# Taking one row of a weight load off half of the DMA engines, and re-cutting the tail of a decode kernel around it

## The chip, the cores and the metric

The kernel runs on one core of a Trainium2 chip. The metric is the device time of one execution in microseconds (us), several executions per kernel. Each execution also lists the *span* of the core, from its first to its last recorded work. Where differences of a few tenths of a microsecond are argued, this document uses medians of spans beside the times.

## The reference, cut to what matters

The kernel computes `x + A(ln(x)) + B(ln(x))` for one token of 1024 values. A is attention over a cache of 65,536 keys with 4 key/value heads and 32 query heads. B is an MLP:

```python
def _B_ref(x, w1, w2, w3, w4):
    ...                                        # x1 = x + a small mixer; with one token the mixer's taps are zero
    h2 = _gelu(_layernorm(x1) @ w3) @ w4       # w3: 1024 x 3584, w4: 3584 x 1024, bf16
    return x1 + h2
```

The cache and the weights are 170 MB, read once. Last comes `w4`: 3584 rows of 1024 bf16 values (2 KB each), 28 rows for each of the 128 SBUF partitions.

## The kernel before

Everything is streamed into three large tiles over one DMA queue. `w4` comes last, in pieces, so that its matmuls can start on the early ones:

```python
W4_PIECES = (8, 12, 5, 2, 1)     # rows per partition of each load, sum 28
FIRST = 3
AT_ONCE = 1
NARROW = 8
AHEAD = 5
...
            elif it == "w4":
                w4_v = B_w4.rearrange("(m c) n -> m c n", c=FC)
                c0 = 0
                for n in W4_PIECES:
                    go(out=t[:, c0 * D:(c0 + n) * D], in_=w4_v[:, c0:c0 + n, :].rearrange("p c n -> p (c n)"))
                    c0 += n
```

A *wide* row is two matmuls of 512 columns, accumulated in the PSUM tile `psB`. The last eight rows are *narrow*: four matmuls of 256 columns in four column groups of the PE array, accumulated in two other PSUM tiles. So two engines copy the result out of PSUM at the end, one half each (0.37 us on ACT and 0.43 on DVE, side by side, for 64x256 values each; the add over 64x512 values that writes `sums` took DVE 0.68). What had been summed in `psB` until then (the other rows, the attention's projection of the last group, the residual) has to be brought over. It is copied to SBUF and added to the narrow tiles by two f32 matmuls with a selection matrix. I call these the *injection*.

```python
    compute_v(NU - 1)
    early = sum(W4_PIECES[:AT_ONCE])
    compute_w4(0, FIRST)
    ...
    projected = project(HKV - 1)
    with tc.issue_after(projected):
        compute_w4(early, FC - NARROW)                        # wide rows
    sums = ogpool.tile([64, 512], F32, name="sums", tag="og")
    nc.vector.tensor_tensor(out=sums[:], in0=psB[0:64, :], in1=tail["o"], op=ALU.add)
    ...
    narrow_rows(FC - NARROW, FC - NARROW + AHEAD, start=True) # the 5-row piece
    ...
    for h in range(2):                                        # the injection
        nc.tensor.matmul(quarters[h][64 * h:64 * h + 64, 0:256], lhsT=pick[:].rearrange("p j r -> p (j r)"),
                         rhs=sums[:, 256 * h:256 * (h + 1)], start=False, ...)
    narrow_rows(FC - NARROW + AHEAD, FC)                      # the 2-row and the 1-row piece
    out_t = ogpool.tile([64, 2, 256], BF16, name="out_t", tag="og")
    nc.scalar.copy(out=out_t[:, 0, :], in_=quarters[0][0:64, 0:256])
    nc.vector.tensor_copy(out=out_t[:, 1, :], in_=quarters[1][64:128, 0:256])
    ...                                                       # store
```

## Time and profile before

| | |
|---|---|
| time, median of the first 3 runs | 401.07 us (400.98 to 402.7) |
| span of the profiled run | 398.6 us |
| load queue, share of 16 engines' time | 98.9% |
| last `w4` landing | 396.44 us |
| start of the last four matmuls | 396.48 us |

The part of the page on DMA queues (queue and kind: packets, megabytes, share of the time of 16 engines) shows what bounds the kernel:

```profile
q1 hardware_dynamic: 4128, 169.87, 98.9%
q8 instruction: 9, 0.15, 0.2%
q14 instruction: 1, 0.01, 0.0%
```

The load queue leaves the DMA engines 1.1% of free time. The other two lines look negligible: nine packets of 16 KB and one of 8 KB. The profile marks all ten as instruction packets (0.98 to 1.10 us for each of the first eight of 16 KB, 0.33 for the one of 8 KB); what the one of 8 KB holds is not shown.

The chain of waits ends like this (start, us, what):

```profile
363.32 33.11 DMA big<-in_B_w_dram
396.44 0.04 issue
396.48 0.34 PE pm_r L501 x4
396.82 0.02 issue
396.84 0.43 DVE out_t L522
```

PE waits for the last load and needs 0.34 us after it. From the start of the last four matmuls to the end of the span are 2.12 us (398.60 - 396.48).

The windows near the end, of which the last two columns are read here (share of the DMA engines that are busy, GB/s):

```profile
394.00:394.50 0.50, 0.25 (x4) 0.00 (x0) 0.21 (x1) 0.00 (x0) 0.00 (x0) 1.00 0.87 344
394.50:395.00 0.50, 0.41 (x16) 0.40 (x20) 0.47 (x1) 0.00 (x0) 0.00 (x0) 1.00 0.55 221
395.00:395.50 0.50, 0.50 (x14) 0.23 (x8) 0.00 (x0) 0.00 (x0) 0.00 (x0) 1.00 0.53 205
395.50:396.00 0.50, 0.50 (x12) 0.17 (x9) 0.00 (x0) 0.00 (x0) 0.00 (x0) 1.00 0.32 119
```

From 394.5 on only about half of the engines still move data (0.55 and 0.53), and then fewer. Each of these loads has 16 landings among the trace's semaphore events, as many as the page counts DMA engines. Read as one landing for each engine, they say which part of them is late. Here are the 16 landings of four loads, as us before the last of the 16 (the trace does not name the engines, the values are sorted):

```
lands at  22.0: 0.63 0.53 0.46 0.43 0.37 0.35 0.34 0.33 0.29 0.26 0.25 0.19 0.18 0.16 0.13 0.00
lands at  50.0: 1.92 1.81 1.74 1.70 1.66 1.63 1.62 1.61 1.57 1.56 1.48 1.47 1.46 1.40 1.30 | 0.00
lands at 166.1: 1.98 1.87 1.81 1.75 1.70 1.69 1.64 1.63 1.55 1.53 1.46 1.38 | 0.72 | 0.18 0.05 0.00
lands at 396.4: 1.96 1.82 1.66 1.54 1.53 1.47 1.37 | 0.71 | 0.31 0.24 0.18 0.17 0.16 0.09 0.05 0.00
```

The first load ends evenly. Then one engine after another falls 1.3 us back (1.30 in the second row), and the eight 16 KB instruction packets before the end (42.5, 105.9, 156.9, 198.0, 253.4, 296.9, 338.0 and 383.8 us) are just as many as the late engines. One engine falls 0.7 us back at the 8 KB packet (113.2 us; of the landings that end at 108.1 us none stands between the two groups, of those that end at 127.4 one does, 0.66 us after the early ones). At the end eight engines are late, one half late, seven early.

### The profile page before, as it was taken

The numbers are of one execution on the slowest core, as the hardware profiler recorded it, in microseconds if no ns is written. First come the engines' busy times: TensorE is split into PE (matmuls) and PEld (weight loads), VectorE is DVE, ScalarE is ACT, GpSimd is POOL, SyncE is SP. The second block draws the span as 40 slices with busy tenths as digits, with TensorE's granted clock in tenths as the row PEclk, the third lists the DMA queues.
The fourth block names the chain that finished last, engine by engine and source line by source line (L and its number), as shares of the span: only waits on it lengthen the run. The fifth ranks groups of instructions, "written<-read, shape, count | busy, mean of one in ns | idle before, by whom it ended". The sixth has DMA issues, their size and how long they took to land.

```text
span 398.6 us, 2575 instructions
## 1 busy us (share of the span) xinstructions
PE 225.4 (57%) x1360; PEld 44.0 (11%) x866; DVE 210.7 (53%) x160; ACT 27.1 (7%) x35; POOL 5.8 (1%) x29
## 2 busy tenths in 40 slices
PE   0251960591569238733974296519462955394986
PEld 0210000010100010011001010200020101010132
DVE  0610010974296559633963795269439942894141
ACT  1001020003000200020002000200110001002000
POOL 2000000000000000000000000000000000000000
PEclk9995996596869787966695889679956896698799
DMA  9998999999999999999999999999999998999996
GB/s 421 421 443 376 446 427 480 454 421 421 416 428 427 421 467 449 427 421 427 423 441 421 447 454 434 416 427 421 441 436 427 447 447 383 416 462 424 413 432 257
DMA packets 4144, 170.03 MB, mean 427 GB/s; under 512 B 419, under 2 KB 421, under 8 KB 678
## 3 DMA queue, kind: packets, MB, share of 16 engines
q1 hardware_dynamic: 4128, 169.87, 98.9%
q8 instruction: 9, 0.15, 0.2%
q14 instruction: 1, 0.01, 0.0%
q10 hardware_dynamic: 6, 0.00, 0.0%
HBM read 169.87 MB, written 0.00 MB: 426 GB/s over the span
## 4 chain that ended last, share of the span: by engine, by line
DMA 56%; DVE 21%; PE 17%; ACT 2%; another core or an unknown queue 2%; issue 1%; SPq 0%; DVEq 0%; ACTq 0%
DMA big<-in_A_k_cache_dram 42%; DVE big L360 15%; PE sc L365 11%; DMA big<-in_B_w_dram 8%; DMA big<-in_A_wq_dram 6%; PE oacc L415 4%; DVE p_sb L386 2%; DVE mx L370 2%; ACT p_sb L383 2%; PE psq L290 1%; SPq L187 0%; PE pm_mx L372 0%; DVE m L374 0%; PE pm_mx L379 0%
## 5 line engine op out<-in xcount | busy, mean ns | idle before, releaser
L365 PE MATMUL sc<-big,qdiag 128*128 128x512 bf16 x512 | 129.6, 414 | 66.5 <-DVE big L360 61.0
L360 DVE STREAM_TRANSPOSE big<-big 128x4096 f32<-128x4096 f32 x32 | 139.4, 4413 | 50.1 <-DMA big<-in_A_k_cache_dram 50.1
L415 PE MATMUL oacc<-big,p_sb 128*32 128x512 bf16 x512 | 43.2, 504 | 34.5 <-DVE p_sb L386 34.5
L370 DVE TENSOR_REDUCE mx<-sc 128x1 f32<-128x2048 f32 x8 | 18.3, 2292 | 29.9 <-PE sc L365 29.9
L365 PEld LDWEIGHTS <-qdiag 128*128 128x128 bf16 x128 | 13.2, 103 | 178.3 <-issue 145.7
L383 ACT ACTIVATE p_sb<-sc,nball 128x2048 bf16<-128x2048 f32 x8 | 15.7, 1968 | 220.8 <-DVE nball L381 220.8
L386 DVE STREAM_TRANSPOSE p_sb<-p_sb 128x2048 bf16<-128x2048 bf16 x8 | 18.5, 2311 | 18.0 <-ACT p_sb L383 18.0
L415 PEld LDWEIGHTS <-p_sb 128*32 128x32 bf16 x512 | 16.2, 122 | 58.2 <-DVE p_sb L386 35.1
L290 PE MATMUL psh<-big,ln_rep_b 128*32 128x512 bf16 (+1 forms) x64 | 12.4, 942 | 8.9 <-DMA big<-in_B_w_dram 8.9
L455 PE MATMUL o_acc<-big,oT 128*1 128x512 bf16 x48 | 13.2, 447 | 2.4 <-ACT p_sb L383 2.4
L372 PE MATMUL pm_mx<-ident_f,mx 128*1 128x128 f32 x8 | 2.4, 296 | 19.1 <-DVE mx L370 19.1
L424 DVE SCALAR_TENSOR_TENSOR og<-oacc,wb,og 128x512 f32<-128x512 f32 x4 | 3.0, 751 | 18.5 <-PE oacc L415 18.5
L329 DVE STREAM_TRANSPOSE h_row<-h_row 128x896 bf16<-128x896 bf16 x1 | 1.1, 1111 | 22.0 <-ACT h_row L328 22.0
L241 PE MATMUL pm_ln<-ln_rowsum_a,ones_f 128*128 128x1 f32 x2 | 0.6, 348 | 12.8 <-DVE ln_rowsum_a L239 12.8
L437 PE MATMUL pm_e<-ol,sel8big 128*128 128x129 f32 x8 | 2.3, 370 | 9.7 <-DVE ol L436 9.7
L314 POOL COPY qdiag<-qx 32x32 bf16<-32x32 bf16 x16 | 3.3, 204 | 278.7 <-PE sc L365 250.7
L290 PE MATMUL psq<-big,ln_rep_a 128*32 128x512 bf16 x64 | 5.0, 479 | 3.7 <-DMA big<-in_A_wq_dram 3.7
L232 DVE STREAM_TRANSPOSE x_t<-x_row 32x256 bf16<-32x256 bf16 x4 | 2.5, 615 | 8.4 <-DMA x_row<-in_A_x_dram 8.3
L466 DVE TENSOR_TENSOR big<-o_acc,big 1x512 f32<-1x512 f32 x2 | 1.4, 679 | 10.3 <-PE o_acc L455 10.3
L227 PE MATMUL psB<-big,hT 128*32 128x512 bf16 x40 | 4.8, 380 | 1.4 <-DMA big<-in_B_w_dram 1.3
L302 DVE CAST q_row<-psq 128x512 bf16<-128x512 f32 x1 | 0.7, 692 | 7.6 <-PE psq L290 7.6
L379 PE MATMUL pm_mx<-ident_f,rep 1*128 1x1 f32 x8 | 1.8, 229 | 5.0 <-DVE rep L376 5.0
(100 smaller groups left out, 71.9 us busy)
## 6 DMA issues: line engine op xcount, KB each, us to landing
big<-in_A_wo_dram SPq DMA_DIRECT2D x1, 8192.0 KB, 35.7
big<-in_B_w_dram SPq DMA_DIRECT2D x1, 7168.0 KB, 38.1
big<-in_B_w_dram SPq DMA_DIRECT2D x3, 2048.0 KB, 35.5
big<-in_B_w_dram SPq DMA_DIRECT2D x1, 3072.0 KB, 29.5
big<-in_B_w_dram SPq DMA_DIRECT2D x1, 1280.0 KB, 32.2
big<-in_B_w_dram SPq DMA_DIRECT2D x1, 512.0 KB
big<-in_B_w_dram SPq DMA_DIRECT2D x1, 256.0 KB, 33.1
big<-in_A_k_cache_dram SPq DMA_DIRECT2D x8, 42.2
```

The lines of the kernel that those rows point to most:

```text
L227: return nc.tensor.matmul(psB[32 * j:32 * j + 32, :], lhsT=lhsT.to_broadcast([lhsT.shape[0], 32]), rhs=rhs, start=start, stop=False, tile_ ...
L232: nc.vector.transpose(out=x_t[32 * a:32 * a + 32].rearrange("p c j -> p (c j)"), in_=x_row[:, 256 * a:256 * (a + 1)].rearrange("p (i c) -> ...
L290: nc.tensor.matmul(acc[32 * q:32 * q + 32, i, 0:n], lhsT=rep[:, c, :], rhs=cols(c, i, q), start=(c == 0), stop=(c == DC - 1), tile_positio ...
L314: nc.gpsimd.tensor_copy(out=qdiag[at, LEAD:].rearrange("p (x c) -> p x c", x=4)[:, :, 32 * a:32 * a + 8], in_=qx[at, :, 8 * g:8 * g + 8])
L360: nc.vector.transpose(out=words, in_=words)
L365: nc.tensor.matmul(sc[:, e, :], lhsT=qdiag[:, c0:c0 + P], rhs=cols[:, s, e, :, b2, :, r], start=(s == 0 and b2 == 0 and r == 0), stop=(s = ...
L370: nc.vector.reduce_max(out=mx[:], in_=sc[:].rearrange("p e n -> p (e n)"), axis=AX.X)
L383: nc.scalar.activation(out=p_sb[:], in_=sc[:], func=ACTF.Exp, bias=nball[:, b:b + 1], scale=SCALE, accum_out=group["lall"][:, b:b + 1])
L386: nc.vector.transpose(out=flat, in_=flat)
L415: mm = nc.tensor.matmul(oacc[32 * q:32 * (q + 1), :], lhsT=pT[:, e, 32 * t:32 * (t + 1)], rhs=vt[:, :, e, t, :], start=(e == 0 and t < 4), ...
L424: nc.vector.scalar_tensor_tensor(out=og[:], in0=oacc[:], scalar=wb[:, 1:2], in1=og[:], op0=ALU.mult, op1=ALU.add)
L455: nc.tensor.matmul(tail["rows"][0:1, h2, :], lhsT=oT[g][:, j:j + 1], rhs=wt[:, g, j, 512 * h2:512 * (h2 + 1)], start=(g == 0 and j == 0), ...
```

## The change

It means to even this out. The 28th row of each partition (128 rows of 2 KB, 8 for each engine) is no longer loaded by all 16 engines. It comes in seven small loads of 3, 3, 3, 5, 8, 8 and 8 partitions (below: the *shares*). The plan counts on a load on k partitions running on k engines, and on the larger of these loads using the engines of the smaller ones too. The engines are numbered here by this nesting alone: 0 to 2 are those of the loads of 3, each larger load adds the next ones, and 8 to 15, the "upper" ones, get no share. So engines 0 to 2 get 25 of the rows, 3 and 4 get 13, 5 to 7 get 9, and 8 to 15 none.

The values of `h` that multiply these scattered rows are put in their places by four small matmuls early on. The tail is re-cut too. The residual is injected before the 12-row piece. Of the sum only the first half is injected, and the second half is added in the final copy. Only six rows are narrow, and the pieces are 9, 12, 5 and 1. The core of the diff:

```diff
-W4_PIECES = (8, 12, 5, 2, 1)
-FIRST = 3
-AT_ONCE = 1
-NARROW = 8
+W4_PIECES = (9, 12, 5, 1)
+LEFT = 4
+SHARES = ((3, 0, 4), (3, 1, 4), (3, 2, 4), (5, 3, 4), (8, 32, 4), (8, 33, 4), (8, 34, 1))
+WHOLE = 27
+FIRST = 6
+NARROW = 6
 AHEAD = 5
...
+                nc.gpsimd.memset(t[:, WHOLE * D:(WHOLE + LEFT + 1) * D].bitcast(F32), 0.0)
+                c0, m0 = 0, 0
+                for share in SHARES[:3] + W4_PIECES[:1] + SHARES[3:] + W4_PIECES[1:]:
...
+                    k, i0, m = share           # k partitions, every fourth from i0, m rows each
+                    go(out=t[i0:i0 + 4 * k:4, WHOLE * D:(WHOLE + m) * D].rearrange("e (i n) -> e i n", i=m),
+                       in_=w4_v[m0:m0 + k * m, WHOLE, :].rearrange("(i e) n -> e i n", e=k))
...
-    nc.vector.tensor_tensor(out=sums[:], in0=psB[0:64, :], in1=tail["o"], op=ALU.add)
...
+    with tc.issue_after(projected):
+        for h in range(2):
+            begun = inject(h, pick[:].rearrange("p j r -> p (j r)"), tail["o"][0:64, 256 * h:256 * (h + 1)], True)
+    with tc.issue_after(begun):
+        compute_w4(early, WHOLE - NARROW)
+    nc.scalar.copy(out=sums[0][:], in_=psB[0:64, 0:256])
+    nc.vector.tensor_copy(out=sums[1][:], in_=psB[0:64, 256:512])
...
+    narrow_rows(WHOLE - NARROW, WHOLE - NARROW + AHEAD)
+    inject(0, ident_f[0:64, 0:64], sums[0][:], False)
+    narrow_rows(WHOLE - NARROW + AHEAD, WHOLE)
...
-    nc.vector.tensor_copy(out=out_t[:, 1, :], in_=quarters[1][64:128, 0:256])
+    nc.vector.tensor_tensor(out=out_t[:, 1, :], in0=quarters[1][64:128, 0:256], in1=sums[1][:], op=ALU.add)
```

More of the change, by code (lines that the diff above doesn't have):

```diff
@@ L126 @@
     assert DH == P and HQ // HKV == 8 and HKV == 4 and D == 1024 and F == 3584 and S == 1
-    assert SK % UKEYS == 0 and sum(W4_PIECES) == FC
+    assert SK % UKEYS == 0 and sum(W4_PIECES) == WHOLE == FC - 1
     NB = SK // UKEYS
@@ L184, in load @@
                 w4_v = B_w4.rearrange("(m c) n -> m c n", c=FC)
-                c0 = 0
-                for n in W4_PIECES:
-                    go(out=t[:, c0 * D:(c0 + n) * D], in_=w4_v[:, c0:c0 + n, :].rearrange("p c n -> p (c n)"))
-                    c0 += n
+                nc.gpsimd.memset(t[:, WHOLE * D:(WHOLE + LEFT + 1) * D].bitcast(F32), 0.0)
+                c0, m0 = 0, 0
+                for share in SHARES[:3] + W4_PIECES[:1] + SHARES[3:] + W4_PIECES[1:]:
+                    if share in W4_PIECES:
+                        go(out=t[:, c0 * D:(c0 + share) * D], in_=w4_v[:, c0:c0 + share, :].rearrange("p c n -> p (c n)"))
+                        c0 += share
+                        continue
+                    k, i0, m = share
+                    go(out=t[i0:i0 + 4 * k:4, WHOLE * D:(WHOLE + m) * D].rearrange("e (i n) -> e i n", i=m),
+                       in_=w4_v[m0:m0 + k * m, WHOLE, :].rearrange("(i e) n -> e i n", e=k))
+                    m0 += k * m
+                assert m0 == P and c0 == WHOLE
             else:
@@ L284 @@
         nc.vector.tensor_copy(out=x_halves[32 * j:32 * j + 1, :], in_=x_row[0:1, 512 * j:512 * (j + 1)])
+    place = ogpool.tile([P, LEFT, P], BF16, name="place", tag="og")
+    nc.gpsimd.memset(place[:], 0.0)
+    m0 = 0
+    for k, i0, m in SHARES:
+        cells = place[:, 0:m, i0:i0 + 4 * k:4].rearrange("p i e -> p e i")
+        nc.gpsimd.affine_select(out=cells, in_=cells, compare_op=ALU.not_equal, fill=1.0, base=-m0,
+                                pattern=[[-1, k], [-k, m]], channel_multiplier=1)
+        m0 += k * m
     def row_matmul(acc, rep, cols, widths):
@@ L316, in place_queries @@
                 in_=qx[at, :, 8 * g:8 * g + 8])
-    hT = const.tile([P, FC], BF16, name="hT")
+    hT = const.tile([P, WHOLE + LEFT], BF16, name="hT")
+    h_left = const.tile([P, 1], BF16, name="h_left")
     def compute_w3():
@@ L329, in compute_w3, with place_left @@
         nc.vector.transpose(out=h_row[:], in_=h_row[:])
-        nc.vector.tensor_copy(out=hT[:], in_=h_row[:, ::32])
+        nc.vector.tensor_copy(out=hT[:, 0:WHOLE], in_=h_row[:, 0:32 * WHOLE:32])
+        nc.vector.tensor_copy(out=h_left[:], in_=h_row[:, 32 * WHOLE:32 * WHOLE + 1])
+    def place_left():
+        pm = ps_M.tile([P, 512], F32, name="pm_h", tag="pm")
+        for x in range(LEFT):
+            nc.tensor.matmul(pm[:, x:x + 1], lhsT=place[:, x, :], rhs=h_left[:],
+                             start=True, stop=True)
+        nc.vector.tensor_copy(out=hT[:, WHOLE:], in_=pm[:, 0:LEFT])
     def compute_w12():
@@ L403, with compute_v @@
     assert NB == 2
-    def compute_v(u):
+    def compute_v(u, fill=None):
         g, b = divmod(u, NB)
@@ L425, in compute_v, with group_rows @@
                                        op0=ALU.mult, op1=ALU.add)
-        group_rows(g, og, ol)
-        return mm.ins
+        group_rows(g, og, ol, fill and (lambda: fill(mm.ins)))
     oT = {}
     tail = {}
-    def group_rows(g, og, ol):
+    def group_rows(g, og, ol, fill):
         pe = ps_M.tile([P, 512], F32, name="pm_e", tag="pm")
@@ L436, in group_rows @@
         nc.vector.tensor_reduce(out=ol[:, 0:DH], in_=og[:].rearrange("p (s d) -> p d s", d=DH), axis=AX.X, op=ALU.add)
-        tail["gathered"] = nc.tensor.matmul(pe[:, 0:DH + 1], lhsT=sel8big[:], rhs=ol[:], start=True, stop=True).ins
+        if fill is None:
+            nc.tensor.matmul(pe[:, 0:DH + 1], lhsT=sel8big[:], rhs=ol[:], start=True, stop=True)
+        else:
+            with tc.issue_after(fill()):
+                tail["gathered"] = nc.tensor.matmul(pe[:, 0:DH + 1], lhsT=sel8big[:], rhs=ol[:], start=True, stop=True).ins
         msk = small.tile([P, 16, 8], F32, name="msk", tag="msk")
@@ L460, in copy_projection @@
     def copy_projection():
-        tail["o"] = st.tiles["w4"][0:64, FC * D:FC * D + D].bitcast(F32)
-        nc.vector.tensor_scalar(out=tail["o"], in0=x_halves[:], scalar1=ln_s1[0:64, 0:1], scalar2=ln_s2[0:64, 0:1],
+        tail["o"] = st.tiles["w4"][:, (WHOLE + LEFT) * D:(WHOLE + LEFT + 1) * D].bitcast(F32)
+        nc.vector.tensor_scalar(out=tail["o"][0:64, :], in0=x_halves[:], scalar1=ln_s1[0:64, 0:1], scalar2=ln_s2[0:64, 0:1],
                                 op0=ALU.mult, op1=ALU.add)
@@ L471, in compute_w4 @@
             for j in range(2):
-                row_acc(j, hT[:, c:c + 1], wt[:, D * c + 512 * j:D * c + 512 * (j + 1)])
+                mm = row_acc(j, hT[:, c:c + 1], wt[:, D * c + 512 * j:D * c + 512 * (j + 1)])
+        return mm.ins
     compute_wq()
@@ L476 @@
     compute_w12()
+    place_left()
     for u in range(NU - 1):
@@ L484 @@
     copy_projection()
-    compute_v(NU - 1)
-    early = sum(W4_PIECES[:AT_ONCE])
-    compute_w4(0, FIRST)
-    with tc.issue_after(tail["gathered"]):
-        compute_w4(FIRST, early)
-    projected = project(HKV - 1)
-    with tc.issue_after(projected):
-        compute_w4(early, FC - NARROW)
-    sums = ogpool.tile([64, 512], F32, name="sums", tag="og")
-    nc.vector.tensor_tensor(out=sums[:], in0=psB[0:64, :], in1=tail["o"], op=ALU.add)
-    quarters = [ps_M.tile([P, 512], F32, name="pm_r", tag="pm") for _ in range(2)]
@@ L497, in quarter_acc, with first_rows @@
-    def quarter_acc(lhsT, rhs, start=False):
-        for h in range(2):
-            for j in range(2):
-                q = 2 * h + j
-                nc.tensor.matmul(quarters[h][32 * q:32 * q + 32, 0:256], lhsT=lhsT(j), rhs=rhs(j, h), start=start, stop=False,
-                                 tile_position=(0, 32 * q), skip_group_check=True)
-    def narrow_rows(lo, hi, start=False):
+    early = W4_PIECES[0]
+    def first_rows(summed):
+        with tc.issue_after(summed):
+            return compute_w4(0, FIRST)
@@ new lines @@
+    compute_v(NU - 1, first_rows)
+    with tc.issue_after(tail["gathered"]):
+        filled = compute_w4(FIRST, early)
+    with tc.issue_after(filled):
+        filled = compute_w4(WHOLE, WHOLE + LEFT)
+    with tc.issue_after(filled):
+        projected = project(HKV - 1)
+    quarters = [ps_M.tile([P, 512], F32, name="pm_r", tag="pm") for _ in range(2)]
+    sums = [ogpool.tile([64, 256], F32, name="sums_a", tag="og"), ppool.tile([64, 256], F32, name="sums_b", tag="p")]
+    pick = small.tile([64, 2, 32], F32, name="pick", tag="msk")
@@ new lines, with inject @@
+    nc.vector.tensor_copy(out=pick[:], in_=ident_f[0:64, 0:64].rearrange("p (j r) -> p j r", r=32)[:, :, 0:1].to_broadcast([64, 2, 32]))
+    def inject(h, lhsT, rows, start):
+        return nc.tensor.matmul(quarters[h][64 * h:64 * h + 64, 0:256], lhsT=lhsT, rhs=rows, start=start,
+                                stop=False, tile_position=(0, 64 * h), skip_group_check=True).ins
+    with tc.issue_after(projected):
+        for h in range(2):
+            begun = inject(h, pick[:].rearrange("p j r -> p (j r)"), tail["o"][0:64, 256 * h:256 * (h + 1)], True)
@@ L505, in narrow_rows @@
+    with tc.issue_after(begun):
+        compute_w4(early, WHOLE - NARROW)
+    nc.scalar.copy(out=sums[0][:], in_=psB[0:64, 0:256])
+    nc.vector.tensor_copy(out=sums[1][:], in_=psB[0:64, 256:512])
+    def narrow_rows(lo, hi):
         wt = st.tiles["w4"]
         for c in range(lo, hi):
-            quarter_acc(lambda j: hT[:, c:c + 1].to_broadcast([P, 32]),
-                        lambda j, h: wt[:, D * c + 512 * j + 256 * h:D * c + 512 * j + 256 * (h + 1)],
-                        start=start and c == lo)
@@ L511 @@
-    narrow_rows(FC - NARROW, FC - NARROW + AHEAD, start=True)
-    pick = small.tile([64, 2, 32], F32, name="pick", tag="msk")
-    nc.vector.tensor_copy(out=pick[:],
-                          in_=ident_f[0:64, 0:64].rearrange("p (j r) -> p j r", r=32)[:, :, 0:1].to_broadcast([64, 2, 32]))
-    for h in range(2):
-        nc.tensor.matmul(quarters[h][64 * h:64 * h + 64, 0:256], lhsT=pick[:].rearrange("p j r -> p (j r)"), rhs=sums[:, 256 * h:256 * (h + 1)], start=False,
-                         stop=False, tile_position=(0, 64 * h), skip_group_check=True)
@@ L518 @@
-    narrow_rows(FC - NARROW + AHEAD, FC)
+            for h in range(2):
+                for j in range(2):
+                    q = 2 * h + j
+                    nc.tensor.matmul(quarters[h][32 * q:32 * q + 32, 0:256], lhsT=hT[:, c:c + 1].to_broadcast([P, 32]),
+                                     rhs=wt[:, D * c + 512 * j + 256 * h:D * c + 512 * j + 256 * (h + 1)], start=False, stop=False,
+                                     tile_position=(0, 32 * q), skip_group_check=True)
+    narrow_rows(WHOLE - NARROW, WHOLE - NARROW + AHEAD)
```

## The prediction

> **What bounds the kernel.** The DMA stream: the DMA view shows the load queue busy for 98.9% of 16 engines' span, 170 MB at 427 GB/s; the chain of waits ends in 33.1 us of w4 loads (363.3 to 396.4), 0.34 us of matmuls, 0.43 us of output copy and the store. Only the last microseconds can move.
>
> **What is unbalanced there.** In windows of 0.25 us the DMA share is 0.83 to 0.98 until 394.5, then about 0.53 until 395.75: half the engines have finished. The 16 landings of the last w4 load agree: seven at 394.47 to 395.07, one at 395.73, eight at 396.13 to 396.44. The first load's spread is only 0.63 us; the late group grows by one engine after each of eight 16 KB packets of the instruction queue (42.5 to 383.8; 1.0 to 1.1 us each). So instruction fetches made the skew. [...] 222 to 320 PE instructions between them.
>
> **What the change does.** It takes the 28th row (2 KB a partition, 8 per DMA engine) off all 16 engines and gives 25, 25, 25, 13, 13, 9, 9, 9 rows to the lowest eight. A 2 KB packet starts every 0.080 us in the last load.
> - Upper eight: 8 rows less, 0.64 us earlier (396.44 to 395.8), if they are the late ones, which the trace does not name.
> - Lowest three: 17 rows more, +1.36 us. They led by 1.4 to 2.0 us, so they now end 0.0 to 0.6 us before the old end.
> So the last landing moves by 0.1 to 0.64 us, about 0.45.
>
> **What it gives back.** Only one row (0.65 us) now lies between the landings of the 5-row and the last piece, before three (394.55 to 396.44). After the 5-row landing PE does 20 narrow matmuls (0.66 us) and one f32 injection (half of 0.58, 0.29), so it reaches the last four matmuls about 0.35 us after the last landing; before it was 0.04. Loss 0.3 us. The output copy becomes an add of 64x256, near the old 0.43.
>
> **Off the critical path.** Pool's zeroing of 128x2560 before the first w4 issue (estimate 2.5 us from 0.54 for 128x536) and eleven w4 issues (0.42 each, some waiting for earlier landings): V's last load covers DMA until 379, the 9-row piece 5.5 us more. Eight more 512-wide matmuls before the last projection (0.9 us; PE had waited 1.3 us for the 12-row piece, which now lands 0.6 later); the residual, now behind the shares, is ready near 390.4, the 12-row piece near 392. 13 more PE instructions make no ninth fetch (188 follow the eighth).
>
> **Prediction.** 0.45 gained less 0.3: about 0.2 us. 400.9 us, 8 in 10 between 400.2 and 401.7; faster by over 2% 0.005, within 2% 0.985, slower by over 2% 0.01.
>
> **What would show it.** The stretch of half DMA share shrinks from 1.3 us to under 0.7; the last load's landings close up; PE works without a gap from the 5-row landing on.
>
> **What would make it wrong.** The early engines are not the lowest eight, or the three with 25 rows not the earliest: the end comes up to 1 us later. A late w4 issue starves the queue near 380. The residual's wait on all shares delays the injection past the 12-row landing. An extra fetch in the tail.

(A clause is cut where marked. No term of the sum goes with it: 0.45 us gained less 0.3, about 0.2. "Lowest" and "upper" are the numbers by nesting from above; that the engines called the lowest are the early ones was the author's assumption.)

## The result

The changed kernel took 401.5 us (median of 6, 401.09 to 401.69), the kernel before 401.05 us beside it (median of 6, 400.88 to 402.7). The ratio is 1.0004, with a 95% interval of 0.9988 to 1.002: the same. (Such a ratio is the mean time of one kernel's runs over that of the other's of the same rounds, so it is not quite the ratio of the medians. Here the single run of 402.7 us hides a part of the difference.) The spans are clearer: 399.0 to 399.3, median 399.05, against a median of 398.7 in three later sets of 9 to 11 runs of the kernel before. So the change costs about 0.35 us of span. That is inside the predicted range, and on the other side of zero from the predicted gain of 0.2. The range reached from a gain of 0.85 us to a loss of 0.65 us, so it held although both terms of the sum were off.

The queues of the changed kernel:

```profile
q1 hardware_dynamic: 4150, 169.87, 98.8%
q8 instruction: 9, 0.15, 0.1%
q14 instruction: 1, 0.01, 0.0%
```

The bytes are the same, with 22 more small packets. The end of its chain of waits:

```profile
380.49 15.15 DMA big<-in_B_w_dram
395.64 0.04 issue
395.68 0.73 PE pm_r L553 x20
396.41 0.57 PE pm_r L536 x2
396.98 0.28 PE pm_r L553 x4
397.26 0.02 issue
397.28 0.42 DVE out_t L563
```

The chain no longer ends with a load. It leaves DMA at 395.64, which is the landing of the 5-row piece, and from there on all is PE: 20 narrow matmuls, the injection, the last four. (The chain counts the work from the end of what came before. By the timeline, the last four start at 396.91.) The same windows as above:

```profile
394.00:394.50 0.50, 0.50 (x8) 0.23 (x4) 0.00 (x0) 0.00 (x0) 0.00 (x0) 1.00 0.76 315
394.50:395.00 0.50, 0.50 (x8) 0.27 (x5) 0.00 (x0) 0.00 (x0) 0.00 (x0) 1.00 0.63 250
395.00:395.50 0.50, 0.36 (x4) 0.06 (x1) 0.00 (x0) 0.11 (x1) 0.00 (x0) 1.00 0.47 176
395.50:396.00 0.50, 0.32 (x12) 0.32 (x15) 0.21 (x1) 0.26 (x1) 0.00 (x0) 1.00 0.13 49
```

The stream ends a little earlier (0.13 in place of 0.32 in the last window), but it still fades over 1.5 us. The landings of the last load, in us before 396.27:

```
2.15 2.02 1.78 | 1.22 | 0.83 0.76 0.66 0.59 0.55 0.51 0.37 | 0.13 0.13 0.10 0.08 0.00
```

The last landing came only 0.17 us earlier (396.44 to 396.27), in one trace of each kernel. And PE, which had started its last four matmuls 0.04 us after the last landing, now starts them 0.64 us after it (396.91 - 396.27). The sum is -0.17 + 0.60 = +0.43 us at the last four matmuls (396.48 to 396.91).

The two timelines of PE from the landing of the 5-row piece on show where the 0.60 comes from. Before:

```profile
394.59 0.73 PE L501 MATMUL pm_r<-big,hT 128*32 128x256 bf16 x20 [0.34 <-DMA big<-in_B_w_dram]
395.25 0.65 PE L516 MATMUL pm_r<-sums,pick 64*64 64x256 f32 x4
395.83 0.40 PE L501 MATMUL pm_r<-big,hT 128*32 128x256 bf16 x8
396.48 0.29 PE L501 MATMUL pm_r<-big,hT 128*32 128x256 bf16 x4 [0.24 <-DMA big<-in_B_w_dram]
```

After:

```profile
395.68 0.73 PE L553 MATMUL pm_r<-big,hT 128*32 128x256 bf16 x20 [0.32 <-DMA big<-in_B_w_dram]
396.34 0.64 PE L536 MATMUL pm_r<-sums_a,ident_f 64*64 64x256 f32 x2
396.91 0.29 PE L553 MATMUL pm_r<-big,hT 128*32 128x256 bf16 x4
```

Before, PE had 1.89 us between the landings of the 5-row and the last piece (394.55 and 396.44) and even waited. After, the two landings are 0.63 us apart (395.64 and 396.27), while PE needs 0.66 us for 20 matmuls and then 0.57 us for the injection. One injection takes 396.34 to 396.91. Two of them had taken 395.25 to 395.83. They stand in different column groups and ran side by side (0.58 us for two, 0.57 for one), so dropping one saved nothing.

### The profile page after: what moved, and what is told of

Same layout as the page of the kernel before. It is cut to its first block, busy times and chain, and to the rows that moved or that the text cites. A ratio compares the mean times of both kernels' runs of the same rounds, so it can differ in the third digit from the quotient of the medians.

```text
span 399.0 us, 2630 instructions
## 1 busy us (share of the span) xinstructions
PE 230.1 (58%) x1368; PEld 45.8 (11%) x874; DVE 210.9 (53%) x162; ACT 27.4 (7%) x36; POOL 10.0 (3%) x38
## 4 chain that ended last, share of the span: by engine, by line
DMA 51%; DVE 23%; PE 19%; ACT 3%; another core or an unknown queue 2%; issue 1%; SPq 0%; DVEq 0%; ACTq 0%
DMA big<-in_A_k_cache_dram 32%; DVE big L387 15%; PE sc L392 11%; DMA big<-in_A_v_cache_dram 10%; PE oacc L442 6%; DMA big<-in_A_wq_dram 5%; DMA big<-in_B_w_dram 4%; DVE p_sb L413 3%; DVE mx L397 3%; ACT p_sb L410 3%; PE psq L308 1%; PE pm_mx L399 0%; DVE m L401 0%; ACT L410 0%
## 5 line engine op out<-in xcount | busy, mean ns | idle before, releaser
L442 PE MATMUL oacc<-big,p_sb 128*32 128x512 bf16 x512 | 45.4, 525 | 34.5 <-DVE p_sb L413 34.5
L237 PE MATMUL psB<-big,hT 128*32 128x512 bf16 x50 | 5.9, 380 | 1.9 <-DMA big<-in_B_w_dram 1.9
L448 ACT COPY og<-oacc 128x512 f32<-128x512 f32 x4 | 2.3, 586 | 33.3 <-PE oacc L442 24.3
```

The source lines that it names most:

```text
L237: return nc.tensor.matmul(psB[32 * j:32 * j + 32, :], lhsT=lhsT.to_broadcast([lhsT.shape[0], 32]), rhs=rhs, start=start, stop=False, tile_ ...
L442: mm = nc.tensor.matmul(oacc[32 * q:32 * (q + 1), :], lhsT=pT[:, e, 32 * t:32 * (t + 1)], rhs=vt[:, :, e, t, :], start=(e == 0 and t < 4), ...
```

## The experiments

Two questions were open. First: is the late end PE work after the 5-row landing (theory P), or are the landings themselves, or the small loads, the cost (rivals D and S)? Second: why did the last landing move by only 0.17 us, and is the fetching of instructions really what makes engines late (theory F), rather than their place (rival U)? Each experiment has a profile. The table is the whole result; "lag" is the time from the last landing to the start of the last four matmuls, "span" the median of all executions of that kernel (six, but five for e9 and e10 and two for e7; of the kernel before, the later sets).

| kernel | 5-row landing | last landing | last four start | lag | span, median | time, median |
|---|---|---|---|---|---|---|
| before | 394.55 | 396.44 | 396.48 | 0.04 | 398.7 | 401.05 |
| changed | 395.64 | 396.27 | 396.91 | 0.64 | 399.05 | 401.5 |
| e1_gap | - | 396.31 | 396.60 | 0.29 | 398.75 | 401.2 |
| e2_bf16 | 396.06 | 396.71 | 396.98 | 0.27 | 399.1 | 401.33 |
| e3_even | 395.75 | 396.39 | 398.19 | 1.80 | 400.3 | 402.33 |
| e4_pieces | 395.89 | 396.53 | 397.17 | 0.64 | 399.2 | 401.48 |
| e5_early | 395.72 | 396.56 | 396.60 | 0.04 | 398.45 | 400.77 |
| e6_level | 396.38 | 397.02 | 397.44 | 0.42 | 399.4 | 401.57 |
| e7_fetch | 395.94 | 397.84 | 397.88 | 0.04 | 400.05 | 402.23 |
| e8_even_early | 395.71 | 396.35 | 396.39 | 0.04 | 398.7 | 400.75 |
| e9_five | 395.76 | 396.40 | 396.45 | 0.05 | 398.7 | 400.76 |
| e10_after_again | 395.60 | 396.22 | 396.87 | 0.65 | 399.0 | 401.61 |

The landings are of one profiled execution each, and they scatter. The five traces with the change's own deal (changed, e1, e2, e5, e10) have their last landing at 396.22 to 396.71, the four with an even deal (before, e3, e4, e8) at 396.35 to 396.53. So the landings alone do not show that the shares made the last one earlier. The spans of most kernels scatter by 0.2 to 0.4 us, apart from single outliers; those of e6 by 0.9. The sets of e1 to e4, of e5 to e8 and of e9 and e10 each ran on a chip of their own, with the kernel before at a median span of 398.7 beside each.

### e1_gap: the old spacing of the last pieces

```diff
-W4_PIECES = (9, 12, 5, 1)
+W4_PIECES = (9, 12, 3, 2, 1)
-AHEAD = 5
+AHEAD = 3
```

> The changed kernel with its 5-row piece cut into 3 and 2 rows (pieces 9, 12, 3, 2, 1; the injection after the 3 rows), so that it has the last-two-pieces spacing of the kernel before; shares kept. Theory P (the end of the changed kernel is PE work that starts at the 5-row landing, 1.27 us of it before the last four matmuls): the last four matmuls again wait for the last landing, which stays near 396.3, and the kernel gains about 0.6 us on the changed one (near 400.85, 0.15 to 0.2 under the kernel before). Rival D (the last landing decides and the shares cost or gain by themselves what was measured): no change from the changed kernel, 401.45.

It gained 0.3 us of span on the changed kernel, half of what theory P expected, and rival D is out. The trace names the missing half. The injection, moved forward, came at 395.80, when its input was just ready (the copy of `psB` had run from 395.38 to 395.74). That copy waits for 24 wide matmuls of 2.77 us that start with the 12-row landing at 392.54. So a second chain, which starts one piece earlier, lay close behind the first. In the kernel before, the 12-row piece had landed at 391.44, because two rows less came before it.

### e2_bf16: a cheaper injection

```diff
-    sums = [ogpool.tile([64, 256], F32, name="sums_a", tag="og"), ...
+    ident_b = const.tile([64, 64], BF16, name="ident_b")
+    nc.vector.tensor_copy(out=ident_b[:], in_=ident_f[0:64, 0:64])
+    sums = [ogpool.tile([64, 256], BF16, name="sums_a", tag="og"), ...
-    inject(0, ident_f[0:64, 0:64], sums[0][:], False)
+    inject(0, ident_b[:], sums[0][:], False)
```

> The changed kernel with the one injected partial sum and its identity in bf16 in place of f32 (rounds the partial sum once more on purpose). Theory P: the injection, 0.57 us from its start to that of the last four matmuls, shrinks to about 0.1 to 0.15, so the last four start near 396.45, and the kernel gains 0.4 to 0.45 us on the changed one (near 401.05, level with the kernel before). Rival D: no change, 401.45.

The time did not move: span 399.1. By its own term the theory held, as the timeline shows:

```profile
396.10 0.73 PE L555 MATMUL pm_r<-big,hT 128*32 128x256 bf16 x20 [0.33 <-DMA big<-in_B_w_dram]
396.76 0.29 PE L538 MATMUL pm_r<-sums_a,ident_b 64*64 64x256 bf16 x1
396.98 0.29 PE L555 MATMUL pm_r<-big,hT 128*32 128x256 bf16 x4
```

From the injection to the last four are 0.22 us, before 0.57. But in this execution the 5-row landing came at 396.06, 0.42 us later than in the profiled run of the changed kernel, and took the gain back. Whether the landings of this build are always that late is not known. Five of its six spans lie between 398.9 and 399.2, so chance in one run would not explain it. A miss for the forecast, and not a decision between the theories.

### e3_even: no shares, the changed tail

```diff
-W4_PIECES = (9, 12, 5, 1)
-LEFT = 4
-SHARES = ((3, 0, 4), ...)
-WHOLE = 27
+W4_PIECES = (10, 12, 5, 1)
+LEFT = 0
+SHARES = ()
+WHOLE = 28
```

(The placing matmuls and their constants go with it.)

> The changed kernel without the shares: all 28 rows even over the engines in pieces of 10, 12, 5, 1, the changed tail kept (one injection, added second half). The last landing should be back at about 396.44 and the 5-row landing at 395.8. Theory P: the end is the 5-row landing plus the same PE work, so last four matmuls near 397.05, 0.15 us later than in the changed kernel (near 401.6). If the shares by themselves cost time (rival S: their small loads or late issues slow the stream), this is faster than the changed kernel, 401.2 or less.

A surprise: five of six executions had spans of 400.3 to 400.5, one had 399.1. The landings are as expected (395.75 and 396.39). The windows of the profiled run show what happened (the column before the DMA share is the granted clock):

```profile
389.00:392.70 3.70, 1.99 (x18) 0.74 (x15) 0.00 (x0) 0.00 (x0) 0.00 (x0) 1.00 0.94 399
392.70:396.10 3.40, 3.39 (x17) 1.35 (x18) 0.00 (x0) 0.00 (x0) 0.00 (x0) 0.50 0.65 267
```

For 3.4 us, from the 12-row landing on, PE ran at half clock (granted 0.50), and the 24 wide matmuls, 2.77 us in e1, took 4.4 us. By the spans this cost about 1.2 us (400.3 against 399.1). In the 3.70 us before, with the wait for the 12-row piece in them, PE had been busy for 1.99. Of the other profiled executions, which paused there too, only that of e6 was caught between its 12-row landing and its last matmuls (below), so what tips it stays open. For the question of this experiment only the single execution of 399.1 counts, which is not enough. It is repeated below, in e4 and e8, with tails that were not throttled (e4: granted clock 1.00 in every window from 384 to 398 us; e8: 24 narrow matmuls in 0.94 us).

### e4_pieces: the kernel before with other pieces

```diff
-W4_PIECES = (8, 12, 5, 2, 1)
+W4_PIECES = (10, 12, 5, 1)
-NARROW = 8
+NARROW = 6
```

> The kernel before with nothing but its pieces changed to 10, 12, 5, 1 (six narrow rows in place of eight). Theory P: losing the two-row piece costs about 0.6 us by itself (near 401.65): 20 narrow matmuls and two injections (0.58 us, as long as the changed kernel's single one) lie between the 5-row landing and the last four matmuls. Equal to e3 within 0.1 us if one injection costs PE as much as two. If dropping one injection saves half of 0.58, as predicted, this is 0.3 us slower than e3.

As theory P expects: moving the two rows of the 2-row piece to the front, and nothing else, makes the kernel before 0.5 us longer (span 399.2 against 398.7), and the lag of the last four is 0.64 us, exactly that of the changed kernel. There are no shares in it and two injections, not one. So the lag of the changed kernel is the price of the piece sizes, and one injection costs PE as much as two:

```profile
395.93 0.73 PE L501 MATMUL pm_r<-big,hT 128*32 128x256 bf16 x20 [0.32 <-DMA big<-in_B_w_dram]
396.59 0.65 PE L516 MATMUL pm_r<-sums,pick 64*64 64x256 f32 x4
397.17 0.29 PE L501 MATMUL pm_r<-big,hT 128*32 128x256 bf16 x4
```

### e5_early: the injection moved into PE's pause

PE waits 1.3 us for the 12-row piece. If all rows after the 9-row piece are narrow, the sum in `psB` is complete before this pause, and the injection fits into it. A narrow row costs PE less than a wide one in these traces: 20 matmuls for five rows in 0.66 us, against 24 matmuls for twelve rows in 2.77 us, so 0.13 against 0.23 us a row.

```diff
-NARROW = 6
+NARROW = 18
...
-    with tc.issue_after(begun):
-        compute_w4(early, WHOLE - NARROW)
...
-    narrow_rows(WHOLE - NARROW, WHOLE - NARROW + AHEAD)
-    inject(0, ident_f[0:64, 0:64], sums[0][:], False)
-    narrow_rows(WHOLE - NARROW + AHEAD, WHOLE)
+    with tc.issue_after(begun):
+        begun = inject(0, ident_f[0:64, 0:64], sums[0][:], False)
+    with tc.issue_after(begun):
+        narrow_rows(WHOLE - NARROW, WHOLE)
```

> The changed kernel, shares and pieces as they are, but with the injection moved off the end: all 18 rows after the 9-row piece go to the four narrow groups (a narrow row took 4 x 36 ns, a wide one 2 x 115 ns), so the partial sum is finished and injected while PE waits for the 12-row piece. Theory P (the late end of the changed kernel is PE work between the 5-row landing and the last four matmuls): the gap from that landing to them falls from 1.27 to about 0.7 us, the last four matmuls start near 396.35, the span goes from 399.05 to 398.5, 0.2 under the kernel before (the part that the shares really bought). Rival D (the landings decide): span stays near 399.05.

It did what theory P says: span 398.45, 0.6 us less than the changed kernel and 0.25 less than the kernel before. In device time the gain on the kernel before is not clear of noise (400.77 against 400.95 beside it, ratio 0.9989 with an interval of 0.9974 to 1.0004). The chain ends with a load again:

```profile
380.91 15.65 DMA big<-in_B_w_dram
396.56 0.04 issue
396.60 0.34 PE pm_r L551 x4
396.94 0.02 issue
396.96 0.43 DVE out_t L562
```

(The profiled execution was the slowest of the six: span 398.7, the others 398.3 to 398.6. Even so its last four matmuls start 0.31 us before those of the changed kernel, although its last load landed 0.29 us later.)

### e8_even_early: the same without the shares

The edit is that of e3 and that of e5 together.

> As e5 without the shares: 28 even rows in pieces 10, 12, 5, 1 with the injection early. Together with e5 it prices the shares alone. Theory: the last landing is back at 396.45, the last four matmuls follow it by at most 0.1 us, span 398.7, equal to the kernel before within 0.1 and 0.2 above e5. If the shares buy nothing, equal to e5; if late PE work did not matter, equal to e3 (399.1 where the clock was not throttled).

Span 398.7, equal to the kernel before and 0.25 us over e5; lag 0.04 us. So a better PE tail alone buys no span, since the kernel before already waited for its last load. The shares alone, freed from the PE tail, seem to buy about 0.25 us of span. They buy nothing in device time, where e5 and e8 are equal (400.77 and 400.75), and in the two profiled executions the last landing of e5 is the later one (396.56 against 396.35). A gain by the shares is therefore not shown.

### e7_fetch: more instructions

```diff
-    nc.at_finalize(keep_loaded_weights)     # the pass that drops repeated weight loads
```

> The kernel before without the pass that drops repeated weight loads: 2675 PE rows in place of 1695, matmuls the same. Theory F (each 16 KB instruction packet makes one DMA engine 1.3 us late, and nothing else made the two groups): 480 to 500 more PE instructions make two more such packets before the end, and the late group has ten engines (or nine with one of them doubly late). Rival U (the upper eight engines are late by their place): eight late engines as before. No use for the time: PE gets 500 more weight loads.

There were ten 16 KB packets before the end in place of eight (the ninth at 348.8 us, the tenth at 384.4 us). The landings of the load that ends at 340.3 us, before the last two, and those of the last load, in us before the last of the 16:

```
lands at 340.3: 1.93 1.92 1.91 1.89 1.77 1.75 1.37 | 0.43 | 0.37 0.19 0.15 0.14 0.13 0.10 0.06 0.00
lands at 397.8: 3.37 3.36 3.35 3.32 3.21 3.20 2.81 | 1.88 | 1.83 1.65 1.62 1.60 1.51 1.45 | 0.07 0.00
```

The two additional packets made no new late engines. They took two that were late already and put them another 1.4 us behind, and the last landing moved from 396.44 to 397.84, by 1.40 us. So theory F holds in its main part: the number of fetches before the end decides how late the latest engine is, at about 1.4 us for each. Its guess that the fetches would walk over ten engines fell. By these landings the ten 16 KB fetches of this run fell on eight engines and left the other eight alone; in that part rival U was right, for no new engine became late.

### Which engines? The changed kernel's own small loads, e10, e6 and e9

A load on 3, 5 or 8 partitions reports 3, 5 or 8 landings, and since the loads are nested, the engines can be told apart. The run e10 is the changed kernel again, unchanged:

> The changed kernel unchanged, on the same chip as e9 and beside the same runs of the kernel before, to price the whole change and the repaired version together: span 399.05, 0.35 us over the kernel before; the small loads on engines 0 to 4 show one early landing out of the two of engines 3 and 4 again, and those on 0 to 7 one early and two late of engines 5 to 7. If another engine is early there, the order of engines is not stable.

```
V cache, 16 engines: 377.15 377.28 377.30 377.38 377.38 377.54 377.62 377.70 | 378.64 | 378.88 378.89 378.94 379.06 379.14 379.16 379.17
first load on 3:     377.63 377.72 377.88
load on 5:           383.02 | 384.16 384.24 384.40 384.46
first load on 8:     383.14 383.36 | 384.43 384.55 384.72 384.73 384.77 384.79
last load, 16:       393.96 394.26 394.57 394.75 | 395.40 395.58 395.62 395.67 395.68 395.68 | 395.86 395.98 396.14 396.15 396.19 396.22
```

Engines 0 to 2 are early: with 4 additional rows each they landed at the height of the early group. In the load on 5 they have 12 additional rows behind them and land at 384.2 to 384.5, as does one of engines 3 and 4, the half late one. The other is early (383.02). The load on 8 repeats these five about 0.33 us later, which leaves three values for engines 5 to 7: one early (383.14) and two late. So the late group is not the upper eight. It is two of engines 5 to 7 and six of the upper ones, and two of the upper ones are early. (This assignment is a deduction from the nesting of the loads. The trace does not name the engines.)

The last load then reads without a rest. Four are early: one of 3 and 4, one of 5 to 7, two upper ones. Six end at 395.40 to 395.68: the late upper engines, relieved of 8 rows. And six end at 395.86 to 396.22: engines 0 to 2 with 25 rows, the half late engine with 13, and the two late ones of 5 to 7 with 9, one more than they had. The change's cost is there again on this chip: span 399.0 against 398.7, time ratio 1.0014 with an interval of 1.0 to 1.0029.

Two other deals of the 128 rows were tried on top of e5:

```diff
-SHARES = ((3, 0, 4), (3, 1, 4), (3, 2, 4), (5, 3, 4), (8, 32, 4), (8, 33, 4), (8, 34, 1))
+SHARES = ((4, 0, 4), (4, 1, 4), (4, 2, 1), (6, 3, 2), (8, 32, 4), (8, 33, 2), (16, 64, 2))     # e6_level
+SHARES = ((3, 0, 4), (3, 1, 4), (3, 2, 2), (5, 3, 4), (5, 32, 4), (5, 33, 2), (16, 64, 3))     # e9_five
```

> As e5, with the same 128 rows dealt 19 each to engines 0 to 3, 10 to 4 and 5, 8 to 6 and 7, and 2 to each upper one, worked out from the landings of the changed kernel's own small loads (engines 0 to 3 and 5 early, 4 half late, 6 and 7 late). If the shares of the changed kernel overshot on engines 0 to 2, the last landing comes about 0.15 us earlier than with them (near 396.1) with a spread of the 16 landings under 1.7 us, and the span is 0.1 to 0.2 under e5. If the late engines move from run to run by more than that, no difference from e5.

This was worse by 0.95 us (span 399.4 against 398.45), in part by a mistake of mine. I had taken engine 4 for the half late one and given engine 3 the full 19 rows. The first load on 4 in this run shows three landings at 377.6 to 377.8 and one at 378.8, so it is engine 3. By that it is the one that landed last, at 397.02, 0.46 us after the last of e5. The rest is the clock: in this execution it was granted at 0.50 from 394.45 us to the end, after 3.4 us in which PE was busy for 1.5. The 24 narrow matmuls from the 5-row landing on took 1.47 us, against 0.94 in e8:

```profile
396.42 1.47 PE L551 MATMUL pm_r<-big,hT 128*32 128x256 bf16 x24 [1.36 <-DMA big<-in_B_w_dram]
395.75 0.94 PE L544 MATMUL pm_r<-big,hT 128*32 128x256 bf16 x24 [1.59 <-DMA big<-in_B_w_dram]
```

That explains the lag of 0.42 us in place of 0.04, and the 2.28 us from the last four matmuls to the end in place of 2.1. How many of the other five executions (spans of 398.8 to 399.5) were throttled is not known.

> As e5 (injection early), with the 128 rows dealt 23 each to engines 0 to 2, 13 each to 3 and 4, and 3 to every other engine, so none of engines 5 to 7 gets more than the upper ones. Theory L (two of engines 5 to 7 belong to the late group and, with 9 rows each, kept the last landing of the changed kernel near its old place[...]): the late engines each get 5 rows less than even, so the last landing comes near 396.05 (396.56 in e5's trace, 396.44 before), no engine below 5 is later than that by over 0.1 us, and the span is 0.1 to 0.3 us under e5's 398.45. Rival (engine order is not stable enough from run to run to be used): no gain on e5, or a loss as in e6.

With engine 3 put right, the landings are level: four early ones, then twelve within 0.36 us. But the last landing was 396.40, not 396.05, with two engines above the ten at 396.04 to 396.19. The span, 398.7, is 0.25 us worse than e5 and no better than the kernel before. So the sums came out for ten of the twelve late or loaded engines, but the other two took more than reckoned, and the change's own deal, read as wrong above, was in fact the best of the three in spans. (In device time e5 and e9 are equal, 400.77 and 400.76, on different chips.) Why e9 loses to e5 is open: the profiled run of e5 landed later (396.56) than that of e9 (396.40), while e5's other executions were shorter. A rival that was not tested is the ninth 16 KB packet. It started after the last landing in the kernel before (397.8) and the changed one (396.6), but before it in e1, e5, e6, e8 and e9 (395.3 to 395.9). In e5 the two latest engines were 0.01 us apart at the 5-row landing and 0.19 at the last one, as if it had held one of them up. The skew at the level of 0.2 us is not settled by these runs.

## Why the prediction was right or wrong

The time, 401.5 us, lies in the predicted range (400.2 to 401.7), and "within 2%" was right. The expected small gain of 0.2 us was a loss of about 0.4 us. The gain came out 0.28 us smaller than predicted and the loss 0.30 us larger; that the range still held is owed to its width, and is luck. Point by point:

- *"The DMA stream" bounds it, "only the last microseconds can move".* Right. In eleven of the twelve traces the span is the start of the last four matmuls plus 2.1 us (2.28 in e6, at half clock). In the changed kernel, though, the chain leaves DMA at 395.64, and the last 1.2 us before that start are PE work.
- *"Instruction fetches made the skew."* Right: e7 added two fetches and 1.40 us. The "222 to 320 PE instructions" between them are 272 on average, from one of the first eight fetches to the next, by the recorded ones in the trace of the kernel before.
- *"Upper eight ... if they are the late ones"; "the last landing moves by 0.1 to 0.64 us, about 0.45".* The size was not right: 0.17 us (0.22 in e10), which is in the range but within the scatter of the landings, as said under the table. By the deduction from e10, six of the upper eight were late, and they gained about what was said (e10: 395.40 to 395.68, before 396.13 to 396.44). Two late engines of the lower eight got a row more and stayed, as did engine 3, half late, with 13 rows. The prediction took the lower engines for the early ones and named this as its first risk.
- *"One f32 injection (half of 0.58, 0.29)".* This is the step that failed. A single injection takes 0.57 us to the start of what follows, because the two of the kernel before had run side by side; halving their common time was wrong. So *"loss 0.3"* was 0.60 (lag 0.04 before, 0.64 after). e4 shows the same lag with two injections.
- The sum with the measured terms is -0.17 + 0.60 = +0.43 us, against -0.45 + 0.3 predicted. Each of the two errors alone would have made a loss of the gain (-0.17 + 0.3, -0.45 + 0.60).
- *The copy with an add "near the old 0.43".* Right: 0.42 us.
- *Off the critical path.* Right in effect: Pool zeroed for 2.23 us (2.5 estimated), the last three loads were issued at 380.0 to 381.4 us, and the DMA share from 378 to 382 us stayed at 0.98 or more. The residual was ready at 390.47 (390.4 predicted). The 12-row piece landed at 392.55, later than the "near 392" of the prediction. It had counted one more row before this piece, but with the shares it is two (as in e4, with ten rows in the first piece, where it landed at 392.81). PE still waited 1.30 us for it. "No ninth fetch" was wrong by the letter: there is one in both kernels (397.8 before, 396.64 after), after the last landing.
- *"PE works without a gap from the 5-row landing on."* As the timeline shows.
- *The stretch of half DMA share "shrinks to under 0.7 us".* Not so. It fades over 1.5 us, because four engines are left early and six are relieved.

## What to carry to other kernels

When loads bound a kernel, look at when each DMA engine lands its part of the last load: here instruction fetches rode on eight of these engines, and each of the first eight put its engine about 1.3 us behind (42.5 to 383.8 us in the kernel before), far from where that was felt, at 396.44. An evening-out by engine pays only if it is known which engines are late, and only if the work after the landing can follow: check what the compute engine needs between the last but one landing and the last. Two operations that overlap do not each cost half of their common time (here 0.58 us for two injections, 0.57 for one), and a step that needs only early data belongs into a pause, not between the last two landings (worth 0.6 us of span here). The whole repaired change, e5, is 0.25 us of span, or 0.06%, under the kernel before, and not clear of noise in time.
